# Eight token tiles of h = x2·w_in by Strassen products in pairs, wo2's blocks packed early and parked in DRAM, attention's steps reordered

## The chip, the cores and the metric

The kernel runs on one core of a Trainium2 chip. The metric is the device time of one launch in microseconds (us). An execution with a hardware profile gives the trace from which all durations below are read. The five engines run their own instruction streams in order and wait for each other by semaphores: PE (TensorE: matmuls and transposes), DVE (VectorE), ACT (ScalarE), POOL (GpSimd) and SP, which here only issues DMA transfers.

## What is computed

```python
x = attention(q, k, v)          # 2 batches, 8 heads, 576 tokens, 64 wide, with rotary angles
x = x.reshape(1152, 512)        # tokens x model width
a, b = x @ w_a, x @ w_b         # 1152 x 1536 each
x2 = (a * b) @ w_out            # 1152 x 512
h = x2 @ w_in                   # 1152 x 1024
solu = h * softmax(h)
ln = layernorm(solu) * g_ln
out = ln @ w_out2               # 1152 x 512
```

The matrices of weights come as 64-bit floats. For float32 accuracy a matmul operand is split in a high part (rounded to the matmul format fp32r) and a low part (the rest), and each product is three matmuls, high·high, high·low and low·high.

## The kernel before

**Order.** The whole program is one table of words, SCHEDULE (lines 36 to 140). A loop at the end of the function looks each word up in STEP or in a second table and calls the step, which emits instructions on its engines. An engine runs what was emitted for it in that order, so the table fixes each queue. A third number in a word (`gl.1.2.1`) puts a step's subtraction on POOL rather than DVE.

**Attention** (0 to 161 us) works on eight units u, each a batch and a pair of heads: loads of q, k and v by SP, rotary "ropes" on POOL and DVE (`rope`, L308, L313, L315; words rq and rk), transposes, scores (qk, L434), row maximum (mx, L443, DVE), exponentials (ex, L451, ACT), transposes of them (tp, L464), their high and low parts (ph on ACT, pl on DVE), and the product with v (pv, L513).

**Weights** come as 64-bit floats. `load_n` fetches one block of 128x1024, `Weights.pack` (L157) builds float32 from the two halves in three instructions of ACT (words pa, pb, pc) and three of DVE (the first, L170, is p2; then p3 and p4), `high` (hi, L181, ACT) writes the rounded part and `low` (lo, L184, DVE or POOL) the rest. Two raw buffers alternate, and `queue` sets the order of blocks: twelve pairs for w_a and w_b, six of w_out, four of w_in (h0 to h3), four of w_out2 (out0 to out3).

**FFN** (161 to 297 us): three of the twelve feature tiles are direct (L704), nine go by seven Strassen products each (`product`, L887).

**X stage** (297 to 378 us): x2 transposed, in three token groups t and twelve steps f. `g_hi` (gh, L936, ACT) and `g_lo` (gl, L734 through the helper tt_) split a·b, `x_mm` (X.t.f, L957) issues twelve matmuls, `x2_hi` (L965) and `x2_lo` (L969) write x2T's parts out of PSUM.

**h stage** (378 us to the end): for each of nine token tiles i of 128 tokens

```python
    def h_mm(i, kk):
        if kk == 0:
            ph[i] = ps_s.tile([P, 2, 512], F32, tag="s", name=f"h{i}")
        for xa, a in ((0, 0), (0, 1), (1, 0)):
            for c in range(2):
                nc.tensor.matmul(
                    ph[i][:, c], x2T[kk][:, xa, i * P:(i + 1) * P], W["h", kk].w[:, a, c * 512:(c + 1) * 512],
                    start=(kk == xa == a == 0), stop=(kk == 3 and xa == 1),
                )
```

that is 24 matmuls of 512 columns a tile (H.i.kk, L981), then the maximum (hx, L988, DVE), exponential (he, L993, ACT), multiplication (hm, L999, DVE), statistics (hs, DVE and one small POOL power, L1009), normalization (hn, L1014, DVE), transposes (L, L1022), their parts (lh on ACT, L1028; ll on DVE), the product with w_out2 (O, L1058) and the store. The four blocks of w_out2 are loaded and packed last, beside the end of the X stage and the start of the h stage.

Of the kernel before, what the change touches and what calls it, by code (L numbers as in the profile page):

```python
# [22 lines left out]
P = 128  # L23
NP = H // 2
# [10 lines left out]
NSTD = 3  # L35
SCHEDULE = """
cs.0 wm1.0 rka0.0 ll.0 rka1.0 rka2.0 kha.0 rqx0.0 rqx1.0 rqx2.0 rqa0.0 rqa1.0 kla.0 rqa2.0 qdx.0 qda.0 wm2.0
kA_0.0 rkb0.0 rkb1.0 kA_1.0 qAx0.0 qA_0.0 qAh0.0 rkb2.0 rqb0.0 lv.0 rqb1.0 khb.0 qAl0.0 R_0.0 qAh1.0 klb.0 R_1.0
R_2.0 wm3.0 qk.0 mx.0 rqb2.0 qdb.0 qAl1.0 wm4.0 qk.1 mx.1 kB_0.0 ex.0 qk.2 qB_0.0 mx.2 rq0.1.1 rk0.1.1 tp.0 ex.1
ex.2 rq1.1.1 kB_1.0 qB_1.0 rk1.1.1 qk.3 rq2.1.1 qk.4 mx.3 rk2.1.1 ex.3 ph.0 mx.4 pl.0 qB_2.0 tp.1 ph.1 t4A_0.0  # L40
t4A_1.0 qd.1 pl.1 qk.5 mx.5 vh.0 tp.2 qA_0.1 tp.3 ex.4 qk.6 kh.1 ph.2 ex.5 t4A_2.0 kl.1.1 t4R_0.0 pl.2 kB_0.1
vl.0.1 ph.3 ld.0 qA_1.1 mx.6 qk.7 qA_2.1 kB_1.1 tp.4 ex.6 pl.3 t4R_1.0 mx.7 lk.2 ph.4 tp.5 kA_0.1 t4R_2.0 R_0.1
rk0.2.1 pl.4 ph.5 pl.5 lq.2 rq0.2.1 qk.8 mx.8 pv00_0.0 rk1.2.1 kA_1.1 tp.6 ex.7 R_1.1 qk.9 R_2.1 rq1.2.1
pv01_0.0 lk.3 rk2.2.1 rq2.2.1 ex.8 qk.10 ph.6 mx.9 qB_0.1 pv00_1.0 pl.6 mx.10 sa.0 lv.1 ex.9 rs_0.0 qB_1.1 qk.11
lv.2 mx.11 pv01_1.0 ex.10 qk.12 lq.3 pv00_2.0 pv00_3.0 tp.7 pv01_2.0 kh.2 kl.2.1 pv01_3.0 qd.2 qB_2.1 mx.12
ex.11 ph.7 pl.7 rs_1.0 rs_2.0 t4B_0.0 qk.13 rk0.3.1 lk.4 tp.8 t4B_1.0 t4B_2.0 mx.13 ex.12 vh.1 ph.8 kA_0.2 tp.9
rk1.3.1 kA_1.2 pl.8 ph.9 pl.9 qk.14 qA_0.2 pv10_0.0 qA_1.2 qA_2.2 vl.1.1 mx.14 tp.10 tp.11 ex.13 pv10_1.0
rk2.3.1 ph.10 ph.11 pl.10 pv11_0.0 pv11_1.0 tp.12 pl.11 ex.14 pv10_2.0 t4R_0.1 pv10_3.0 qk.15 pv11_2.0 pv11_3.0
rq0.3.1 rq1.3.1 kB_0.2 t4R_1.1 ph.12 t4A_0.1 kh.3 kB_1.2 t4R_2.1 rq2.3.1 qd.3 t4A_1.1 qk.16 pl.12 tp.13 tp.14
mx.15 mx.16 pv00_0.1 kl.3.1 t4A_2.1 ex.15 qk.17 ph.13 pl.13 R_0.2 pv00_1.1 ph.14 pl.14 ex.16 tp.15 mx.17 R_1.2  # L50
# [1093 lines left out]
```

## Time and profile before

| | us |
|---|---|
| three runs | 485.25, 485.4, 486.24; median 485.4 |
| profiled execution | 484.92 |
| its span, first to last instruction | 483.1 |
| PE busy | 472.3 (98%) |
| DVE busy | 390.6 (81%) |
| ACT busy | 332.4 (69%) |
| POOL busy | 172.2 (36%) |

Busy times are sums over instructions; the granted TensorE clock was 0.99 to 1.00 of full speed throughout. The stretches in the rows further down are stages of the program, and a chain is followed back from the last instruction, each step to what released it.

### The profile page before, as it was taken

The numbers are of one execution on the slowest core, as the hardware profiler recorded it, in microseconds if no ns is written. First come the engines' busy times: TensorE is split into PE (matmuls) and PEld (weight loads), VectorE is DVE, ScalarE is ACT, GpSimd is POOL, SyncE is SP. The second block draws the span as 40 slices with busy tenths as digits, with TensorE's granted clock in tenths as the row PEclk, the third lists the DMA queues.
The fourth block names the chain that finished last, engine by engine and source line by source line (L and its number), as shares of the span: only waits on it lengthen the run. The fifth ranks groups of instructions, "written<-read, shape, count | busy, mean of one in ns | idle before, by whom it ended". The sixth has DMA issues, their size and how long they took to land.

```text
span 483.1 us, 8335 instructions
## 1 busy us (share of the span) xinstructions
PE 472.3 (98%) x3132; PEld 446.4 (92%) x3132; DVE 390.6 (81%) x582; ACT 332.4 (69%) x619; POOL 172.2 (36%) x138
## 2 busy tenths in 40 slices
PE   7899999999999999999999999999999999999997
PEld 7789999999989999999999999999999878888886
DVE  5789999999999898988886878786777888587441
ACT  4799999999998375777666668576767576133312
POOL 1999989969316002022221532020321202010000
PEclk9999999999999999999999999999999999999999
DMA  5642333421002523222422134423423200000012
GB/s 123 172 128 74 100 82 102 114 65 50 27 28 86 166 68 117 88 87 89 135 81 61 74 94 168 176 87 121 143 95 139 115 1 2 22 24 22 24 42 67
DMA packets 45779, 41.76 MB, mean 86 GB/s; under 512 B 23787, under 2 KB 40746, under 8 KB 45226
## 3 DMA queue, kind: packets, MB, share of 16 engines
q1 hardware_dynamic: 44794, 40.33, 27.0%
q10 hardware_dynamic: 944, 0.89, 0.6%
q8 instruction: 25, 0.41, 0.4%
q14 instruction: 16, 0.13, 0.1%
HBM read 36.92 MB, written 2.39 MB: 81 GB/s over the span
## 4 chain that ended last, share of the span: by engine, by line
PE 82%; DVE 10%; DMA 2%; issue 2%; POOL 2%; ACT 2%; SPq 1%; ACTq 0%; DVEq 0%; POOLq 0%
PE x L957 14%; PE out L1058 10%; PE pb L887 9%; PE ab L704 8%; PE h L981 7%; PE s L434 6%; PE pv L513 6%; PE pc L887 6%; PE pa L887 6%; PE t L464 5%; DVE nm L443 2%; PE lt L1022 2%; DMA kraw<-in_k_dram 1%; DVE pT L482 1%; DVE f L174 1%
## 5 line engine op out<-in xcount | busy, mean ns | idle before, releaser
L957 PE MATMUL x<-gs,wx 128*128 128x384 f32 x432 | 75.4, 334 | 0.0
L957 PEld LDWEIGHTS x<-gs,wx 128*128 128x128 f32 x432 | 74.9, 188 | 0.2
L434 PE MATMUL s<-kS,qS 128*128 128x288 f32 x320 | 59.6, 311 | 3.1 <-DVE qS L384 1.4
L443 DVE TENSOR_REDUCE nm<-s 128x1 f32<-128x576 f32 x72 | 54.0, 752 | 5.1 <-PE s L434 4.2
L451 ACT ACTIVATE e<-s,nm 128x576 f32<-128x576 f32 x72 | 53.7, 746 | 4.6 <-DVE nm L443 4.3
L164 ACT ACTIVATE f<-f 128x1024 f32<-128x1024 f32 x48 | 50.9, 1064 | 0.9
L981 PE MATMUL h<-wh,x2T 128*128 128x512 f32 x216 | 51.2, 392 | 0.2 <-DVE et L999 0.2
L434 PEld LDWEIGHTS s<-kS,qS 128*128 128x128 f32 x320 | 45.1, 188 | 6.1 <-ACT e L451 2.8
L482 DVE TENSOR_TENSOR pT<-t,pT 128x512 fp32r<-128x512 f32 x72 | 48.4, 684 | 0.8
L981 PEld LDWEIGHTS h<-wh,x2T 128*128 128x128 f32 x216 | 40.1, 188 | 8.6 <-PE h L981 0.6
L513 PE MATMUL pv<-pT,V 128*128 128x288 f32 x288 | 46.5, 301 | 0.0
L464 PE MATMUL t<-ident,e 128*128 128x128 f32 x288 | 42.6, 274 | 0.6 <-DVE pT L482 0.3
L478 ACT CAST pT<-t 128x512 fp32r<-128x512 f32 x72 | 41.2, 586 | 1.6 <-PE t L464 1.1
L513 PEld LDWEIGHTS pv<-pT,V 128*128 128x128 f32 x288 | 39.9, 188 | 0.5
L1058 PE MATMUL out<-wo,lnT 128*128 128x512 f32 (+1 forms) x180 | 39.8, 373 | 0.0
L1028 ACT CAST lnT<-lt 128x512 fp32r<-128x512 f32 x18 | 10.2, 589 | 40.6 <-PE lt L1022 40.6
L704 PE MATMUL ab<-xT,wab 128*128 128x384 f32 x216 | 38.1, 335 | 0.0
L734 POOL TENSOR_TENSOR gs<-g,gs 128x384 fp32r<-128x384 f32 x15 | 17.7, 1181 | 55.7 <-ACT gs L936 55.7
L704 PEld LDWEIGHTS ab<-xT,wab 128*128 128x128 f32 x216 | 37.4, 188 | 0.0
L464 PEld LDWEIGHTS t<-ident,e 128*128 128x128 f32 x288 | 33.9, 140 | 2.5 <-DVE pT L482 1.1
L1058 PEld LDWEIGHTS out<-wo,lnT 128*128 128x128 f32 x180 | 31.0, 189 | 5.3
L172 DVE SCALAR_TENSOR_TENSOR f<-raw,f 128x1024 int32<-128x1024 int32 x26 | 34.8, 1340 | 0.4
(181 smaller groups left out, 992.0 us busy)
## 6 DMA issues: line engine op xcount, KB each, us to landing
raw<-in_moe_w_out_dram SPq DMA_DIRECT2D x10, 1024.0 KB
raw<-in_moe_w_a_dram SPq DMA_DIRECT2D x12, 512.0 KB
raw<-in_moe_w_b_dram SPq DMA_DIRECT2D x24, 256.0 KB
raw<-in_moe_w_in_dram SPq DMA_DIRECT2D x4, 1024.0 KB
kraw<-in_k_dram SPq DMA_DIRECT2D x16, 128.0 KB
qd<-in_q_dram SPq DMA_DIRECT2D x16, 128.0 KB
vraw<-in_v_dram SPq DMA_DIRECT2D x8, 256.0 KB
qd<-qd SPq DMA_DIRECT2D x6, 288.0 KB
```

The lines of the kernel that those rows point to most:

```text
L164: act.activation(_raw(t), _raw(t), AF.Copy, scale=2.0 ** -SHIFT)
L434: nc.tensor.matmul(s[:, c, :KC], qS[u % 2][:, a, off:off + P], kS[u % 2][:, h, c * KC:(c + 1) * KC], start=(m == 0), stop=(m == last),)
L443: nc.vector.tensor_reduce(t, ps[n][:, :, :KC], axis=AX.XY, op=ALU.max, negate=True)
L451: nc.scalar.activation(t.rearrange("p (c n) -> p c n", c=2), ps.pop(n)[:, :, :KC], AF.Exp, bias=nm.pop(n), accum_out=sums[u][:, i:i + 1],)
L464: nc.tensor.transpose(t[:, j, :], e[n][:, j * P:(j + 1) * P], ident)
L482: nc.vector.tensor_tensor(lo, src, _raw(hi), op=ALU.subtract)
L513: nc.tensor.matmul(o[:, :KC], w[:, h, 4 if m == 8 else m % 4].rearrange("p a d -> p (a d)"), t[:, m, c * KC:(c + 1) * KC], start=(m == 0), ...
L704: nc.tensor.matmul(pab[f, t][:, m, :CW], wf[:, a, (kk, 4 + (kk + 2) % 4)[m], :], xT[kk][:, xa, t * CW:(t + 1) * CW], start=(kk == a == xa ...
L887: nc.tensor.matmul(dst[:, c, :KC], w[:, a, k * P:(k + 1) * P], x(k, xa)[:, c * KC:(c + 1) * KC], start=(fresh and k == a == xa == 0), stop ...
L957: nc.tensor.matmul(px[t, m][:, :CW], w[:, a], r[:, ga], start=(f == 0 and a == ga), stop=(f == NF - 1 and a == 1),)
L981: nc.tensor.matmul(ph[i][:, c], x2T[kk][:, xa, i * P:(i + 1) * P], W["h", kk].w[:, a, c * 512:(c + 1) * 512], start=(kk == xa == a == 0), ...
L1058: nc.tensor.matmul(po[i, part][:, cols], lnT[i][:, la, kk, :], w[:, a, cols], start=(kk == la == a == 0), stop=(kk == NK2 - 1 and la == 1),)
```

## The change

**h in pairs.** Tile 0 stays as it was (L1038). Tiles (1,2), (3,4), (5,6) and (7,8) go by Strassen: with the two tiles' rows, the two halves of the 512-wide sum and the two halves of h's 1024 columns as 2x2 blocks, seven products Q1 to Q7 (`h_product`, L1131) of 6 matmuls each give both tiles. The weight sums T are built once (`ht_sum`, words u1 to u4 on DVE, tile tfh; high parts `ht_hi`, L1060, ACT). Their low parts are made without a vector engine: ACT writes the negated high part (`ht_seed`, L1067), and a DMA issued by POOL adds the sum onto it (`ht_add`, L1070), four transfers of 512 KB from SBUF to SBUF. The sums S of x2's blocks are built for each pair (`hs_sum`, tile sf, DVE and POOL) and split (`sx_hi`, L1104, ACT; `sx_lo`). The first tile of a pair ends in PSUM (ph), the second in SBUF (hs), by two ACT copies and two DVE additions. One extra matmul (L1114) stands ahead of the first pair.

**w_out2 early.** out0 and out1 are loaded among the FFN's blocks, out2 and out3 ahead of w_in's. After packing and scaling, SP writes each as 512 KB to DRAM (`spill`, so, L784) and brings it back later (`bring`, ri, L789); `high_there` and `low_there` split it then.

**Buffers and order.** a·b's tile is six of two instead of two of six, x2T one tile, and all words of SCHEDULE stand in a new order, attention's too; four ropes move from POOL to DVE.

```diff
-rk0.2.1 pl.4 ph.5 pl.5 lq.2 rq0.2.1 qk.8 mx.8 pv00_0.0 rk1.2.1 kA_1.1 tp.6 ex.7 R_1.1 qk.9 R_2.1 rq1.2.1
+kA_0.1 kA_1.1 ex.7 qk.8 t4R_2.0 R_0.1 rq0.2.1 rk1.2 mx.8 pv00_0.0 R_1.1 qk.9 pv00_1.0 pl.4 ph.5 tp.6 rk2.2.1
...
-    queue = [("ab", f) for f in range(NF)]
-    queue += [("x", n) for n in range(6)] + [("h", n) for n in range(4)] + [("out", n) for n in range(4)]
+    queue = [("ab", f) for f in range(10)] + [("out", 0), ("ab", 10), ("out", 1), ("ab", 11)]
+    queue += [("x", n) for n in range(6)] + [("out", 2), ("out", 3)] + [("h", n) for n in (0, 2, 1, 3)]
...
+    def spill(n):
+        t = W[queue[n]].t
+        spilled[n] = dram.tile([P, 8 * P], F32, tag="wd", name=f"wd{n}", bufs=4)
+        nc.sync.dma_start(out=spilled[n], in_=_raw(t))
+
+    def bring(n):
+        w = W[queue[n]]
+        w.w = home(n)
+        nc.sync.dma_start(out=_raw(w.w[:, 1]), in_=spilled[n])
...
+            b11, b12, b21, b22 = (_raw(W["h", 2 * r + k].t)[:, c * 512:(c + 1) * 512] for r in range(2) for c in range(2))
+            dst, x, y = {1: (0, b12, b11), 3: (1, b22, b12), 2: (2, b22, t[:, 0]), 4: (3, b21, t[:, 2])}[j]
+            tt_(t[:, dst], x, y, sub, eng)
...
+    def ht_seed(k, j):
+        nc.scalar.activation(hT[k, j][:, 1], _raw(hT[k, j])[:, 0], AF.Copy, scale=-1.0)
+
+    def ht_add(k, j):
+        nc.gpsimd.dma_start(
+            out=_raw(hT[k, j])[:, 1].rearrange("p a n -> p (a n)"),
+            in_=tf2[k][:, 2 * j:2 * j + 2].rearrange("p a n -> p (a n)"), accum_op=ALU.add,
+        )
...
+            for k in range(2):
+                for xa, a in ((0, 0), (0, 1), (1, 0)):
...
+                    nc.tensor.matmul(
+                        dst, l, w, start=(fresh and k == xa == a == 0), stop=(k == 1 and xa == 1), skip_group_check=True
+                    )
...
+    def q_add(c):
+        def fn(i):
+            src = ph[i][:, 1] if c else pc2.pop(i)
+            nc.vector.tensor_tensor(hs[i][:, c], src, hs[i][:, c], op=plus)
+            if c:
+                ph[PAIRS[i]] = hs[i]
...
+        "Q1": h_product("a", (0, 0), (0, 0), True), "Q2": h_product("a", (1, 0), (1, 0)),
+        "Q3": h_product("b", 4, (1, 1)), "Q4": h_product("c", (1, 1), 4), "Q5": h_product("b", 1, 1),
+        "Q6": h_product("b", 2, 2), "Q7": h_product("c", 3, 3, True),
```

On PE, at the passage from the X stage to the h stage, the kernel before goes on with whole tiles (h_4709 is tile 1, h_4735 tile 2; gs is a·b's part, wh a block of w_in):

```order
L957 MATMUL x_3_4468<-gs_11_4617,wx_4269 128x384 x3
L981 MATMUL h_4709<-wh_4388,x2T_4414 128x512 x6
L981 MATMUL h_4709<-wh_4395,x2T_4416 128x512 x6
L981 MATMUL h_4709<-wh_4569,x2T_4411 128x512 x6
L981 MATMUL h_4709<-wh_4582,x2T_4422 128x512 x6
L981 MATMUL h_4735<-wh_4388,x2T_4414 128x512 x6
```

and the changed one runs tile 0 (h_4752), the extra matmul and the first products of the pair (h_4789 is tile 1, hc the third accumulator, hT the weight sums, sx the sums S):

```order
L1013 MATMUL x_3_4511<-gs_11_4670,wx_4231 128x384 x3
L1038 MATMUL h_4752<-wh_4493,x2T 128x512 x6
L1038 MATMUL h_4752<-wh_4655,x2T 128x512 x6
L1038 MATMUL h_4752<-wh_4519,x2T 128x512 x6
L1038 MATMUL h_4752<-wh_4672,x2T 128x512 x6
L1114 MATMUL h_4789<-wh_4493,x2T 128x512
L1131 MATMUL h_4789<-wh_4493,x2T 128x512 x3
L1131 MATMUL h_4789<-wh_4655,x2T 128x512 x3
L1131 MATMUL hc_4804<-hT_4523,sx_4740 128x512 x3
L1131 MATMUL hc_4804<-hT_4726,sx_4740 128x512 x3
L1131 MATMUL h_4789<-hT_4633,sx_4740 128x512 x3
L1131 MATMUL h_4789<-hT_4735,sx_4740 128x512 x3
```

Tile 0, which the kernel before has among the last steps of the X stage, comes behind it, and the weight sums hT_4726 and hT_4735 are wanted by the fourth and the sixth group behind tile 0.

On ACT the changed kernel makes those weight sums' parts at that passage (CAST on L1060 the high part, ACTIVATE on L1067 the negated copy, L1022 x2T's high parts, L992 a·b's, L192 w_in's):

```order
L1060 CAST hT_4633<-tfh_4490 128x1024
L1067 ACTIVATE hT_4633<-hT_4633 128x1024
L992 CAST gs_9_4638<-g_3725 128x384
L992 CAST gs_10_4652<-g_3921 128x384
L192 CAST wh_4655<-f 128x1024
L992 CAST gs_11_4670<-g_3921 128x384
L192 CAST wh_4672<-f 128x1024
L1022 ACTIVATE x2T<-x_0_4499 128x384
L1060 CAST hT_4726<-tfh_4721 128x1024
L1022 ACTIVATE x2T<-x_2_4507 128x384
L1067 ACTIVATE hT_4726<-hT_4726 128x1024
L1060 CAST hT_4735<-tfh_4721 128x1024
```

Behind it comes the negated copy for hT_4735; in the kernel before, ACT packs w_out2 at this place. POOL issues the adding DMA behind each negated copy.

On POOL, at the start of attention, the kernel before has these ropes (t2q and t2k the swapped products, qd and kraw the results, of units 0 and 1):

```order
L344 TENSOR_TENSOR kd_178<-kraw_104,kd_178 128x4x64
L315 TENSOR_TENSOR qd_105<-qd_105,t2q_0_215 128x4x64
L308 TENSOR_TENSOR t2q_1_285<-qd_168,s_sb 128x576
L308 TENSOR_TENSOR t2k_1_287<-kraw_172,s_sb 128x576
L313 TENSOR_TENSOR qd_168<-qd_168,c_sb 128x9x64
L313 TENSOR_TENSOR kraw_172<-kraw_172,c_sb 128x576
L315 TENSOR_TENSOR qd_168<-qd_168,t2q_1_285 128x9x64
L315 TENSOR_TENSOR kraw_172<-kraw_172,t2k_1_287 128x576
```

and the changed one these:

```order
L327 TENSOR_TENSOR qd_102<-qd_102,t2q_0_210 128x4x64
L356 TENSOR_TENSOR kd_169<-kraw_101,kd_169 128x4x64
L325 TENSOR_TENSOR qd_159<-qd_159,c_sb 128x9x64
L327 TENSOR_TENSOR kraw_163<-kraw_163,t2k_1_270 128x576
L327 TENSOR_TENSOR qd_159<-qd_159,t2q_1_258 128x9x64
```

Both swapped products and k's product with the cosines of unit 1 are DVE's now (of unit 2, one more).

## Rows read from the trace of the kernel before

**Rows 1.** Busy time of each engine by stage (length, PE PEld DVE ACT POOL, clock, DMA share, GB/s).

```profile
0.00:20.00 20.00, 16.09 (x116) 14.57 (x116) 11.87 (x29) 10.96 (x28) 10.20 (x14) 1.00 0.65 171
20.00:80.00 60.00, 58.26 (x466) 55.53 (x467) 56.67 (x97) 57.54 (x146) 56.70 (x45) 1.00 0.36 95
80.00:161.00 81.00, 79.62 (x630) 75.65 (x630) 78.79 (x134) 73.80 (x184) 48.71 (x39) 1.00 0.22 59
161.00:297.50 136.50, 136.50 (x965) 136.35 (x965) 116.66 (x147) 93.69 (x121) 30.12 (x17) 1.00 0.33 109
297.50:366.00 68.50, 68.50 (x397) 68.50 (x396) 50.45 (x59) 49.21 (x70) 14.66 (x13) 1.00 0.35 124
...
378.00:440.00 62.00, 61.78 (x293) 51.12 (x292) 48.96 (x77) 29.46 (x45) 9.18 (x8) 1.00 0.04 15
440.00:483.10 43.10, 39.52 (x213) 33.69 (x211) 18.07 (x32) 9.99 (x19) 1.65 (x3) 0.99 0.14 39
```

**Rows 2.** Chain that ended last, from the X stage on (start, length, what).

```profile
297.54 68.66 PE x L957 x396
...
402.04 5.46 PE h L981 x24
...
471.03 8.50 PE out L1058 x60
```

**Rows 3.** Groups by line and shape: busy us, mean ns, idle before.

```profile
L172 DVE SCALAR_TENSOR_TENSOR f<-raw,f 128x1024 int32<-128x1024 int32 x26 | 34.8, 1340 | 0.4
...
L174 DVE SCALAR_TENSOR_TENSOR f<-raw,f 128x1024 int32<-128x1024 int32 x26 | 33.3, 1281 | 0.5
...
L170 DVE TENSOR_SCALAR f<-f 128x1024 int32<-128x1024 int32 x26 | 20.6, 795 | 7.5 <-ACT f L164 7.5
...
L734 DVE TENSOR_TENSOR gs<-g,gs 128x384 fp32r<-128x384 f32 x21 | 12.5, 600 | 7.6 <-ACT gs L936 7.6
...
L1014 DVE TENSOR_SCALAR et<-et,mv,rs 128x1024 f32<-128x1024 f32 x9 | 9.4, 1039 | 2.9 <-POOL rs L1009 2.9
...
L965 ACT ACTIVATE x2T<-x 128x384 fp32r<-128x384 f32 x12 | 5.5, 488 | 0.9 <-PE x L957 0.9
L734 DVE TENSOR_TENSOR tf<-f 128x512 f32<-128x512 f32 x8 | 5.5, 690 | 0.3
...
L734 DVE TENSOR_TENSOR tf<-f,tf 128x256 f32<-128x256 f32 x13 | 5.5, 420 | 0.2
...
L184 DVE TENSOR_TENSOR wh<-f,wh 128x1024 fp32r<-128x1024 f32 x4 | 4.9, 1218 | 0.2 <-ACT wh L181 0.2
...
L181 ACT CAST wh<-f 128x1024 fp32r<-128x1024 f32 x4 | 4.2, 1052 | 0.0
```

**Rows 4.** POOL's timeline early in attention (start, length, engine, instruction).

```profile
12.13 1.41 POOL L308 TENSOR_TENSOR t2q<-qd,s_sb 128x576 f32<-128x576 f32 x1
...
18.99 1.42 POOL L315 TENSOR_TENSOR kraw<-kraw,t2k 128x576 f32<-128x576 f32 x1
```

**Rows 5.** SP's timeline: one block of w_out, 1 MB, is issued.

```profile
353.70 0.38 SPq L229 DMA_DIRECT2D raw<-in_moe_w_out_dram  x1
```

**Rows 6.** Busy time by microsecond behind that issue, columns as in rows 1.

```profile
354.00:355.00 1.00, 1.00 (x8) 1.00 (x7) 0.56 (x1) 0.58 (x2) 0.35 (x1) 1.00 0.09 33
...
356.00:357.00 1.00, 1.00 (x7) 1.00 (x6) 0.58 (x2) 1.00 (x3) 0.00 (x0) 1.00 1.02 422
...
358.00:359.00 1.00, 1.00 (x8) 1.00 (x7) 0.96 (x2) 0.81 (x2) 0.51 (x1) 1.00 0.01 4
```

**Rows 7.** Chain that ended last, in attention: a small transfer.

```profile
69.17 2.50 DMA rd<-rr
```

**Rows 8.** DVE's timeline at one place of the h stage.

```profile
381.29 2.89 DVE L1014 TENSOR_SCALAR et<-et,mv,rs 128x1024 f32<-128x1024 f32 x1 [0.67 <-POOL rs L1009]
```

**Rows 9.** POOL's timeline at the same place.

```profile
381.23 2.41 POOL L184 TENSOR_TENSOR wo<-f,wo 128x1024 fp32r<-128x1024 f32 x1
```

**Rows 10.** Waits of 0 to 161 us (total, times, longest).

```profile
DVE nm L443 <- PE s L434: 4.2, 8, 0.8
```

More of the change, by code (lines that the diff above doesn't have):

```diff
@@ L46 @@
[L46 to L50, printed above, removed]
@@ L199, in attention_gated_ffn_solu_ffn @@
     xp = ctx.enter_context(tc.tile_pool(name="xp", bufs=1))
-    xT = [xp.tile([P, 2, NT], F32R, tag=f"x{m}", name=f"xT{m}") for m in range(NP)]
+    x_all = xp.tile([P, NP, 2, NT], F32R, tag="x", name="xT")
+    xT = [x_all[:, m] for m in range(NP)]
     NF = DF1 // P
@@ L726, in to_ffn @@
         pools["a"] = sctx.enter_context(tc.tile_pool(name="ps_a", bufs=1, space=PSUM))
[L727 to L728 removed]
+        for f in range(0, 6, 2):
+            g_tile(f)
+        sums_f = [gpool.tile([P, 2, 2, S], F32, tag=f"g{3 + j}", name=f"sums_f{j}") for j in range(3)]
         sums_x = sp.tile([P, 3, 2, 2, S], F32R, tag="s", name="sums_x")
@@ L962, in x2_hi @@
     def x2_hi(t, m):
-        if x2T[m] is None:
-            x2T[m] = xp.tile([P, 2, NT], F32R, tag=f"x{m}", name=f"x2T{m}")
+        if not x2T:
+            pools["x2"] = x2 = xp.tile([P, 4, 2, NT], F32R, tag="x", name="x2T")
+            x2T.extend(x2[:, k] for k in range(4))
         nc.scalar.activation(x2T[m][:, 0, t * CW:(t + 1) * CW], px[t, m][:, :CW], AF.Copy, scale=UP ** -2)
@@ new lines, in attention_gated_ffn_solu_ffn, with sx_src, sx_dst, sx_hi @@
+    SX = {3: 2, 2: 0, 1: 1, 4: 3}
+    def sx_src(i, q):
+        return sf[i][:, q in (1, 4), :, q != 4]
+    def sx_dst(i, q, a):
+        return sx[i][:, SX[q], a].rearrange("p (k n) -> p k n", k=2)
+    def sx_hi(i, q):
+        if i not in sx:
+            sx[i] = pools["l"].tile([P, 4, 2, 2 * P], F32R, tag="S", name=f"sx{i}", bufs=1)
+        nc.scalar.copy(sx_dst(i, q, 0), sx_src(i, q))
+    def sx_lo(i, q, eng=0):
+        tt_(sx_dst(i, q, 1), sx_src(i, q), _raw(sx_dst(i, q, 0)), sub, eng)
@@ new lines, in h_product @@
+    def h_product(name, left, right, fresh=False):
+        def fn(i):
+            if name == "a" and fresh:
+                ph[i] = ps_s.tile([P, 2, 512], F32, tag="s", name=f"h{i}")
+                if i == min(PAIRS):
+                    nc.tensor.matmul(ph[i][:, 1], x2T[0][:, 0, 0:P], W["h", 0].w[:, 0, 0:512], start=True, stop=True)
+            if name == "c" and fresh:
+                pc2[i] = ps_o.tile([P, 512], F32, tag="o", name=f"hc{i}")
+            dst = pc2[i] if name == "c" else ph[i][:, "ab".index(name)]
+            for k in range(2):
+                for xa, a in ((0, 0), (0, 1), (1, 0)):
+                    if isinstance(left, int):
+                        l = sx[i][:, SX[left], xa, k * P:(k + 1) * P]
+                    else:
+                        h, second = left
+                        r = (PAIRS[i] if second else i) * P
+                        l = x2T[2 * h + k][:, xa, r:r + P]
+                    if isinstance(right, int):
+                        w = hT[k, right in (2, 4)][:, a, right in (3, 4)]
+                    else:
+                        h, c = right
+                        w = W["h", 2 * h + k].w[:, a, c * 512:(c + 1) * 512]
+                    nc.tensor.matmul(
+                        dst, l, w, start=(fresh and k == xa == a == 0), stop=(k == 1 and xa == 1), skip_group_check=True
+                    )
+        return fn
@@ new lines, in q_seed, with q_copy, fn @@
+    def q_seed(i):
+        nc.scalar.copy(ph[i][:, 1], ph[i][:, 0])
+    def q_copy(c):
+        def fn(i):
+            if i not in hs:
+                hs[i] = pools["h"].tile([P, 2, 512], F32, tag="hs", name=f"hs{i}")
+            nc.scalar.copy(hs[i][:, c], pc2[i] if c else ph[i][:, 1])
+        return fn
+    def q_add(c):
+        def fn(i):
+            src = ph[i][:, 1] if c else pc2.pop(i)
+            nc.vector.tensor_tensor(hs[i][:, c], src, hs[i][:, c], op=plus)
+            if c:
+                ph[PAIRS[i]] = hs[i]
+        return fn
```

305 lines of the change are left out of this document (187 added, 118 removed).

## The prediction, made before the run

> **What bounds the kernel now.** I read the busy times by stage first, then the chain, then the durations by shape, then single places of the timelines.
>
> By stage [rows 1], PE is busy for 136.50 of 136.50 us in the FFN, 68.50 of 68.50 in the X stage and 61.78 of 62.00 in the h stage up to 440 us. The last window has 39.52 us of matmuls, and the chain's last piece of PE, 8.50 us from 471.03 [rows 2], ends at 479.53: that window too is full until PE has nothing left. From 161 us to the end PE's own work is the bound, and what leaves PE there leaves the time, as long as nothing makes it wait. In attention PE is busy for 153.97 of 161 us, DVE for 147.33 [rows 1]; from 20 us on DVE idles only 3.33 + 2.21 = 5.5 us, of which 4.2 behind scores [rows 10]. There DVE and PE bound together, and POOL is full until 80 us (56.70 of 60).
>
> The time is the profiled execution's: 484.92, span 483.1. The median of the three runs, 485.4, stands 0.48 above it; I add that at the end. About 0.2% (1.0 us) is what a measurement of this kernel can tell from no change.
>
> **Part 1: fewer matmuls in h.** Before, nine tiles of 24 make 216. After, tile 0 has 24, four pairs have 7 products of 6, that is 168, and one extra stands ahead: 193, so 23 less. They have the same 512 columns. In the chain 24 of them take 5.46 us [rows 2], 0.2275 each: 23 x 0.2275 = **5.2 us** off PE, all of it in the part that PE bounds.
>
> **Part 2: the sums that pay for it.** Per pair, DVE and POOL build 8 sums S and 4 low parts, ACT 4 high parts and three copies, DVE two additions of 128x512 (0.69 [rows 3]). All four blocks of w_out2 are packed earlier; a block costs DVE 0.80 + 1.34 + 1.28 = 3.42 us [rows 3]. DVE by stage: the FFN takes in two blocks (6.8) and some four low parts and products that POOL had, about 1 us each: from 116.7 [rows 1] to about 127.6, of 136.5 of PE. The X stage takes in the weight sums, 8 x 0.69 = 5.5, and a few more low parts (0.60, 1.22 [rows 3]): from about 56 to 64, of 75 up to tile 0's maximum. The h stage loses two packings (6.8) and gains 8 additions (5.5) and some 5 us of sums: from about 71 to 74, of 98. ACT grows by 14 and 11 us in the first two stages and stays at least 20 under PE in the FFN; in X it comes to 74 with 75 there, where not all of it is due at X's end. POOL goes from about 11 us in the last two windows [rows 1] to 27.5. Every engine stays under PE in each stage, so I price these sums at nothing; the cover is 9 us of DVE in the FFN, which would be gone if DVE ran 7% slower there.
>
> **Part 3: the passage from X to h.** Before, tile 0's matmuls lay among X's last ones. Now they come behind them, and the second half of the weight sums is made just there. Count from the end of X's last matmul. X's matmuls take 68.66/396 = 0.173 us each [rows 2]. PE then has four groups of 6 for tile 0 (5.45 us), the extra one and Q1 (1.6), one group on hT_4523 (0.7): **hT_4726 is wanted at 7.7 us, hT_4735 at 9.1.** On ACT, the first high part of x2T waits for nine matmuls before the end (-1.56) and takes 0.49 [rows 3]; then high part 1.05, x2T 0.49, negated copy 1.05, high part 1.05, copy 1.05 [rows 3]: the two adding DMAs can be issued at about 1.5 and 3.6. DVE has the sums ready in time: it starts 24 matmuls before the end (-4.2), where a ring buffer comes free, and needs 0.69, 0.42 and four times 0.69, so it ends near -0.3. From issue to landing, then, **6.2 and 5.5 us are covered by PE's own work.**
>
> What such a DMA takes no row shows: POOL issues none in this trace. Bounds: a small transfer took 2.50 us [rows 7]; 1 MB issued at 353.70 [rows 5] had its last byte by about 358.0 [rows 6], 4.4 us, of which 1.2 us was before the first byte and the rest at up to 422 GB/s. An adding transfer of 512 KB moves its bytes three times (two reads, one write): 1.5 MB at that rate is 3.7, and with 1.2 ahead about 5. So 2.5 to 5; I take 4.4, the nearest row by bytes, which is under the cover: **no stall.** The Trainium skill ("DMA: Bandwidth & Descriptors", section on the anatomy of a DMA of the software path) puts such a transfer at about 2.0 us + bytes/436 GB/s; by that it would be an estimated 3.2 us, and the sum the same.
>
> Smaller waits are there by the order: the copy of Q1's result for a seed stands behind the exponential of tile 0 on ACT (about 0.3 of wait on PE), tile 3's first product waits until tile 0's multiplication frees PSUM (about 0.2), and some 0.3 for the other pairs. These are guesses from 0 to 2; I take **+0.8.** At the end, tile 8's normalization is ready some 14 us after the last product (two tiles' maximum to normalization in series on DVE, the last of PE's sums in SBUF) and its transposes come at 15.4 in PE's order, 1.4 us later: nothing.
>
> **Part 4: w_out2 through DRAM.** Four writes and four reads of 512 KB, beside a DMA share of 0.33 to 0.35 [rows 1]. The first block is wanted by a matmul more than 15 us after its read is issued, against 4.4 for a transfer of 1 MB: nothing. SP has little behind these issues but stores.
>
> **Part 5: attention's order.** Four ropes leave POOL (4 x 1.42 = 5.7 us), which has them without a gap from 12.13 to 20.4 us [rows 4]. On DVE they cost about 0.75 each (a sum of 512 columns takes 0.69 [rows 3], a rope has 576), 3.0 in all; three of the four fall between 12 and 20 us, where DVE idles (11.87 of 20 busy [rows 1]), one where it doesn't. The matmuls, maxima and exponentials are the same, only interleaved otherwise. Against: at most the 3.0. For: at most what waits for POOL until 80 us, some 3 to 4 of PE's 3.91 + 1.74 = 5.7 idle us there [rows 1]. I take **0**, and keep -3 to +3.
>
> Sum: 484.92 - 5.2 + 0.8 + 0 = 480.5; with the 0.48 above, **481.0 us.**
>
> **Rivals.**
>
> (a) *The adding DMAs land late, and the change is slower.* The two tiles that they read from share one buffer: the second half's sums on DVE wait until the first half's DMAs have landed, and the second half's DMAs follow. The first pair is issued between 9 and 7.4 us before the end of X. A landing time L within 5 us costs nothing; beyond, both delays add, and PE stalls about 2L - 11. The gain of 4.4 is gone, and this decides, from L = 8 us on; with L = 10 it is +9, **490.** For it: no row has such a transfer, DVE and POOL work without a pause there. Against: 1 MB took 4.4.
>
> (b) *Attention's order costs more than 3 us.* DVE idles only 5.5 us from 20 us on; an order in which maxima come later behind scores doubles the 4.2 us of that wait [rows 10], and with the rope about +5: **486.** Against it, PE's and DVE's streams are otherwise the same.
>
> (c) *Attention gains more than 3 us.* POOL, full until 80 us, was what loads and keys waited for; with 5.7 us less there PE's idle time shrinks: -4, **477.**
>
> (d) *DVE and POOL disturb each other.* Where both ran, DVE's normalization took 2.89 us [rows 8] beside a subtraction of POOL of 2.41 [rows 9]; the other eight average (9.4 - 2.89)/8 = 0.81 [rows 3]. POOL's work in the h stage grows two and a half times. Eight such meetings are up to 17 us on DVE, which idles 13 us until 440 [rows 1] and 25 behind; so most is covered, and 1 to 3 us show at the passage or at the end: **483.** The Trainium skill ("SBUF — State Buffer", section "Who interferes with whom") says that a DVE instruction in its two-port mode and GpSimd block each other fully, and that one with two SBUF inputs contends with GpSimd's reads; the pair of rows agrees with the first, and by the second the new sums S, all from SBUF, would meet too.
>
> (e) *It doesn't save what it counts*: PE idles for the seeds and additions of each pair, four times 1.5 us: **486.**
>
> **How the numbers follow.** Forecast (478 to 484): 0.63, nearly all faster by over 0.2% (0.62, and 0.01 same). (a) 0.11: 0.03 faster, 0.02 same, 0.06 slower. (b) 0.08: 0.02 same, 0.06 slower. (c) 0.07, faster. (d) 0.06: 0.04 faster, 0.01 each of the others. (e) 0.05: 0.01 same, 0.04 slower. Sum: faster 0.76, same 0.07, slower 0.17. The range leaves out about half of (a) and little of the rest above, and the far end of (c) below: **476.5 to 487.0.**
>
> **What would show it.** The first matmul of X at the same time as before within 3 us (part 5). h's matmuls at 193 and PE some 5 us shorter. Behind X's last matmul, PE without a pause over 0.5 us up to the first product on hT_4735, and the second half's adding DMAs landing within 5.5 us of their issue (part 3). DVE under PE in the FFN, with X's start as far from the end of attention as before, 136.4 us (part 2). The prediction is wrong if the FFN and X stages get longer by over 2 us, if PE has stalls of over 2 us before the pairs' products, or if attention moves by over 3.

## The result and the profile after

The change made the kernel slower: 488.48 us (median of six runs, 488.14 to 490.23) against 485.48 (six runs, 485.05 to 486.24), a ratio of 1.0061 with a 95% interval of 1.0043 to 1.0079. The forecast was 481.0, with a range of 476.5 to 487.0. The profiled execution took 488.67, its span is 486.6, against 484.92 and 483.1 before.

By stage the changed kernel reads as follows (busy time of each engine; columns as in [rows 1], the last four windows cut where its stages lie):

```profile
0.00:20.00 20.00, 17.17 (x122) 15.81 (x122) 14.81 (x34) 11.79 (x30) 6.89 (x12) 1.00 0.54 124
20.00:80.00 60.00, 58.12 (x464) 55.28 (x465) 57.91 (x97) 57.26 (x145) 53.73 (x42) 1.00 0.40 105
80.00:161.00 81.00, 79.01 (x624) 74.70 (x623) 78.28 (x134) 72.74 (x183) 50.27 (x40) 1.00 0.23 63
161.00:297.50 136.50, 135.15 (x951) 134.23 (x950) 122.93 (x152) 100.73 (x130) 26.45 (x18) 1.00 0.39 129
297.50:371.00 73.50, 73.50 (x428) 73.36 (x428) 56.66 (x73) 60.25 (x84) 16.66 (x13) 1.00 0.49 155
371.00:396.00 25.00, 21.18 (x94) 17.66 (x93) 22.80 (x29) 12.10 (x20) 14.55 (x14) 0.93 0.41 106
396.00:440.00 44.00, 43.43 (x210) 35.86 (x209) 38.92 (x65) 20.09 (x39) 19.52 (x19) 1.00 0.05 19
440.00:486.60 46.60, 42.65 (x227) 36.38 (x225) 27.22 (x47) 14.66 (x29) 7.38 (x10) 1.00 0.13 34
```

Attention takes as long as before. Two stages that were full on PE no longer are: the FFN, 135.15 of 136.50 us, and the passage to the h stage, 21.18 of 25.00 and the only stretch with a granted clock under full speed (0.93). Before, the stretch of the passage was:

```profile
371.00:396.00 25.00, 24.78 (x119) 20.96 (x118) 21.80 (x33) 16.84 (x24) 3.49 (x3) 1.00 0.23 85
```

PE's timeline of the changed kernel shows where (start, length, matmuls; in brackets what the group waited for):

```profile
239.03 1.85 PE L943 MATMUL pc<-xT,wT 128*128 128x288 f32 x12 [0.63 <-ACT p L956]
...
287.87 1.85 PE L943 MATMUL pb<-xT,wB 128*128 128x288 f32 x12 [0.52 <-DVE p L972]
289.93 1.86 PE L943 MATMUL pa<-xT,wB 128*128 128x288 f32 x12 [0.20 <-ACT pb L952]
...
299.76 0.51 PE L1013 MATMUL x<-gs,wx 128*128 128x384 f32 x2
...
374.64 5.64 PE L1038 MATMUL h<-wh,x2T 128*128 128x512 f32 x24
380.12 0.39 PE L1114 MATMUL h<-wh,x2T 128*128 128x512 f32 x1
...
381.71 1.52 PE L1131 MATMUL hc<-hT,sx 128*128 128x512 f32 x6
387.05 2.31 PE L1131 MATMUL h<-hT,sx 128*128 128x512 f32 x6 [3.82 <-ACT h L1138]
389.16 3.87 PE L1131 MATMUL h<-wh,x2T 128*128 128x512 f32 x12
392.87 1.52 PE L1131 MATMUL h<-hT,sx 128*128 128x512 f32 x6
...
409.50 0.66 PE L1193 MATMUL lt<-ident,et 128*128 128x128 f32 x4 [0.57 <-DVE et L1185]
```

With the same marks in the trace of before, the difference of the spans, 3.5 us, is accounted for:

| from, to (on PE) | before | after | difference |
|---|---|---|---|
| start to the first Strassen product of the FFN | 192.67 | 192.67 | 0 |
| to the first matmul of X | 104.71 | 107.09 | +2.4 |
| to the end of X and tile 0's h | 80.42 | 80.36 | -0.1 |
| to the last matmul | 101.73 | 102.55 | +0.8 |
| to the end | 3.57 | 3.90 | +0.3 |

What stands behind the second line shows at the first of the three waits in the FFN. On ACT the read-out that PE waits for (L956, word o7.6, 0.64 us) stands behind the high part of a weight sum (L890, word th.7):

```profile
237.40 1.05 ACT L890 CAST wT<-tf 128x1024 fp32r<-128x1024 f32 x1
238.34 0.64 ACT L956 COPY p<-pc 128x576 f32<-128x576 f32 x1
```

The fourth line of the table hides two large terms. The 23 matmuls that are gone are 5.2 us; against them stand the wait of 3.82, a clock that fell behind it (the 18 matmuls from 387.05 to 392.87 took 5.82 us, where 18 x 0.2275 would be 4.1: 1.7 more), and the wait of 0.57: 6.1 together.

**What PE waited for at 387.05.** The product Q6 of the first pair adds onto a copy that ACT makes (L1138). On ACT the copy stands behind the exponential of tile 0, that one waits for tile 0's maximum on DVE, and on DVE the maximum stands behind a sum of x2's blocks, S2b (L747, sf). DVE's timeline there:

```profile
378.67 0.42 DVE L747 TENSOR_TENSOR sx<-sf,sx 128x256 fp32r<-128x256 f32 x1
379.19 4.95 DVE L747 TENSOR_TENSOR sf<-sf,x2T 128x256 f32<-128x256 f32 x1
384.06 1.21 DVE L1159 TENSOR_REDUCE mx<-h 128x1 f32<-128x1024 f32 x1
```

and POOL's:

```profile
378.62 0.88 POOL L1070 DMA_DIRECT2D hT<-tfh  x1 [0.20 <-POOL sf L747]
379.23 1.59 POOL L747 TENSOR_TENSOR sf<-x2T 128x512 f32<-128x512 f32 x1
380.49 1.03 POOL L747 TENSOR_TENSOR sx<-sf,sx 128x256 fp32r<-128x256 f32 x1
381.18 2.67 POOL L747 TENSOR_TENSOR wout<-wout 128x1024 fp32r<-128x1024 f32 x1
384.22 0.72 POOL L747 TENSOR_TENSOR sf<-x2T,sf 128x256 f32<-128x256 f32 x1 [0.37 <-DVE sf L747]
```

A DVE sum of 256 columns, 0.43 us for the same step of the second pair, lasted 4.95: it began 40 ns ahead of three POOL instructions without a gap and ended 0.3 us after the last of them. The instructions of both engines read two operands from SBUF each. And just ahead of that run POOL had issued the last adding DMA, which was then in flight. So there are two suspects: POOL's run and the DMA.

The adding DMAs themselves landed in time. In the page's list of DMA issues the last column is the median from issue to landing:

```profile
hT<-tfh POOLq DMA_DIRECT2D x4, 512.0 KB, 5.0
```

The four took 4.6 to 5.4 us. The last one, issued at 378.62, landed at 383.76, 5.1 us later, under the 5.5 that PE's work was to cover.

### The profile page after: what moved, and what is told of

It reads as the page before. It is cut to its first block, busy times and chain, and to the rows that moved or that the text cites. A ratio compares the mean times of both kernels' runs of the same rounds, so it can differ in the third digit from the quotient of the medians.

```text
span 486.6 us, 8468 instructions
## 1 busy us (share of the span) xinstructions
PE 470.2 (97%) x3109; PEld 443.3 (91%) x3109; DVE 419.5 (86%) x624; ACT 349.6 (72%) x655; POOL 195.5 (40%) x164
## 4 chain that ended last, share of the span: by engine, by line
PE 69%; DVE 14%; ACT 5%; POOL 3%; DMA 3%; issue 3%; SPq 0%; ACTq 0%; POOLq 0%; DVEq 0%
PE x L1013 15%; PE out L1229 10%; PE ab L716 8%; PE pb L943 7%; PE pc L943 5%; PE pa L943 5%; PE h L1131 5%; PE pv L525 5%; PE s L446 4%; PE t L476 3%; DVE nm L455 2%; DVE sf L747 2%; DVE pT L494 2%; PE lt L1193 2%; PE hc L1131 1%
## 5 line engine op out<-in xcount | busy, mean ns | idle before, releaser
L446 PE MATMUL s<-kS,qS 128*128 128x288 f32 x320 | 58.6, 309 | 1.6 <-ACT e L463 1.6
L1229 PE MATMUL out<-wout,lnT 128*128 128x512 f32 (+1 forms) x240 | 51.8, 372 | 0.0
L1229 PEld LDWEIGHTS out<-wout,lnT 128*128 128x128 f32 x240 | 41.3, 189 | 7.2
L179 DVE SCALAR_TENSOR_TENSOR f<-raw,f 128x1024 int32<-128x1024 int32 x26 | 32.3, 1244 | 0.5
L747 POOL TENSOR_TENSOR gs<-g,gs 128x384 fp32r<-128x384 f32 x10 | 10.9, 1090 | 53.2 <-ACT gs L992 34.3
L177 DVE SCALAR_TENSOR_TENSOR f<-raw,f 128x1024 int32<-128x1024 int32 x26 | 31.8, 1221 | 0.4
L943 PE MATMUL pa<-xT,wB 128*128 128x288 f32 x216 | 31.7, 295 | 0.2 <-ACT pb L952 0.2
L943 PE MATMUL pb<-sums_x,wT 128*128 128x288 f32 x216 | 31.6, 295 | 0.0
```

The costliest lines, as they stand in the source:

```text
L446: nc.tensor.matmul(s[:, c, :KC], qS[u % 2][:, a, off:off + P], kS[u % 2][:, h, c * KC:(c + 1) * KC], start=(m == 0), stop=(m == last),)
L943: nc.tensor.matmul(dst[:, c, :KC], w[:, a, k * P:(k + 1) * P], x(k, xa)[:, c * KC:(c + 1) * KC], start=(fresh and k == a == xa == 0), stop ...
L1229: nc.tensor.matmul(po[i, part][:, cols], lnT[i][:, la, kk, :], w[:, a, cols], start=(kk == la == a == 0), stop=(kk == NK2 - 1 and la == 1),)
```

## Experiments at the passage: POOL's run or the DMA

Theory A: POOL's back-to-back sums hold DVE up. Rival B: the adding DMAs do.

**POOL emptied (a_pool_empty).** In SCHEDULE, three POOL steps go behind S4a and S4b, which wait for S2b:

```diff
-hx.0 Sh.1.2 S1a.3.1 Sl.1.1.1 he.0 Sl.1.2 xl.2.1 Q1.1 ri.10 lj.12.1 q1.1 S4a.1.1 hj.10 S4b.1.1 Q7.1
+hx.0 Sh.1.2 he.0 Sl.1.2 xl.2.1 Q1.1 ri.10 q1.1 S4a.1.1 hj.10 S4b.1.1 Sl.1.1.1 S1a.3.1 lj.12.1 Q7.1
```

> Three POOL steps (S1a.3, Sl.1.1 and the low part of w_out2's block, lj.12) stand behind S4b.1 instead of ahead of it, so that POOL has nothing to run while DVE makes S2b of the first pair. Theory A (DVE's sum of two SBUF tiles is held up by POOL's back-to-back sums): that sum takes 0.4 to 0.6 us instead of 4.95, PE's wait ahead of Q6 of the first pair falls from 3.8 to under 0.5 us, the clock stays up, the time falls by about 5 us, to 483 to 484. Rival B (the adding DMAs, landing at that time, hold DVE up): the sum still takes 3 to 5 us and the time stays within 1.5 us of 488.5.

Measured: 484.06 us (10 runs) against 485.47 for the kernel before in the same series, ratio 0.9968 (0.9953 to 0.9983). DVE's sum, with the DMAs as they were:

```profile
378.94 0.43 DVE L741 TENSOR_TENSOR sf<-sf,x2T 128x256 f32<-128x256 f32 x1
```

PE has no wait at all ahead of Q6 and the clock of 371 to 396 us is 1.00. One move of three words gives 4.4 us back by the medians; from X's first matmul to the last matmul the two traces have 177.9 us against 182.9, 5.0 less. POOL's run is necessary for the hold-up.

**The longest of the three moved (b_lj_late).** Only `lj.12.1` goes behind `S4b.1.1`.

> Only the longest of the three POOL steps, lj.12 (2.67 us), is moved behind S4b.1. Theory A: DVE's sum ends when POOL's Sl.1.1 does, so it takes about 2.3 us instead of 4.95, PE's wait falls by about 2.7 us to some 1.2, the time to 484 to 486. Rival B: the sum stays at 3 to 5 us and the time within 1.5 us of 488.5.

Measured: 485.6 us, ratio 1.0001 (0.9986 to 1.0016). DVE's sum and POOL's two instructions:

```profile
379.33 2.62 DVE L741 TENSOR_TENSOR sf<-sf,x2T 128x256 f32<-128x256 f32 x1
```
```profile
379.37 1.60 POOL L741 TENSOR_TENSOR sf<-x2T 128x512 f32<-128x512 f32 x1
380.63 1.02 POOL L741 TENSOR_TENSOR sx<-sf,sx 128x256 fp32r<-128x256 f32 x1
```

Here too the sum ends 0.3 us behind POOL's run, of two instructions now, and not with the last adding DMA, which landed at 383.92. PE's wait is 1.49 us and the clock doesn't fall.

**Without the DMAs (c_no_dma).** The negated copies go and two subtractions on DVE take the DMAs' place:

```diff
-un.1.0 S1a.1 ua.1.0 S1b.1 uh.1.1 un.1.1 S2a.1.1 lo.25 Sh.1.3 Sh.1.1 ua.1.1
+S1a.1 ul.1.0 S1b.1 uh.1.1 S2a.1.1 lo.25 Sh.1.3 Sh.1.1 ul.1.1
```

> The second half's two adding DMAs and negated copies are replaced by two subtractions on DVE (1.2 us each); POOL's other steps stay. Theory A: DVE's S2b of the first pair still ends only when POOL's run of sums ends, so it takes over 1.5 us wherever the two overlap, and PE's wait stays at 3 us or more. Rival B: with no DMA in flight the sum takes 0.4 to 0.6 us.

Measured: 488.88 us in one run. The sum took 0.78 us, though POOL ran one instruction beside it and the next behind; but DVE's own 2.4 us of subtractions came later instead, PE waited 0.95 and 2.23, and nothing was gained. It moved both engines' times and did not settle the question.

**The DMAs left out, all else in place (e_no_add).** The words `ua.1.0` and `ua.1.1` are deleted; the pairs of h then lack the weight sums' low parts.

> The second half's two adding DMAs are left out (the negated high parts stay where the low parts should be, so h's pairs lose that correction); POOL's run of sums and DVE's order stay. Theory A in its plain form (POOL's back-to-back sums alone hold DVE up): DVE's S2b of the first pair takes over 3 us as before, PE waits over 2.5 us ahead of Q6, the time is 487 to 489. Rival B' (POOL's run holds DVE up only while an adding DMA is in flight or being issued): the sum ends at the first boundary between POOL's instructions, under 2 us, and the time falls to 484 to 486.

Measured: 485.81 us in one run. DVE's sum and POOL's same three instructions:

```profile
381.26 0.78 DVE L741 TENSOR_TENSOR sf<-sf,x2T 128x256 f32<-128x256 f32 x1
```
```profile
379.57 1.30 POOL L741 TENSOR_TENSOR sf<-x2T 128x512 f32<-128x512 f32 x1
380.82 0.93 POOL L741 TENSOR_TENSOR sx<-sf,sx 128x256 fp32r<-128x256 f32 x1
381.71 2.58 POOL L741 TENSOR_TENSOR wout<-wout 128x1024 fp32r<-128x1024 f32 x1
```

It began inside POOL's second instruction and got in at that one's end, although the third followed at once. DVE's step just ahead of it, a low part of the same size (0.42 in the changed kernel), began inside POOL's first instruction and got in at that one's end:

```profile
379.79 1.37 DVE L741 TENSOR_TENSOR sx<-sf,sx 128x256 fp32r<-128x256 f32 x1
```

So theory A in its plain form fell: the run alone costs DVE one instruction of POOL, not three. But without the DMAs the run also began earlier, so DVE's sum started inside it rather than just ahead of it.

**The start moved (h_phase).** One word, `xl.2.1`, goes ahead of `S2b.1`, so that DVE's sum starts inside POOL's first instruction, with the DMAs in place.

> One word is moved: DVE writes a low part of x2T (xl.2.1, 0.5 us) ahead of the first pair's S2b instead of behind it, so that S2b begins inside POOL's first sum instead of 40 ns ahead of it; the adding DMAs and POOL's run stay. Theory A' (a DVE sum that begins inside a POOL instruction gets in at that one's end, one that begins just ahead of POOL's run waits for all of it): S2b takes 0.9 to 1.7 us, PE's wait ahead of Q6 falls from 3.8 to 0.5 to 1.5 us, the time to 484 to 485.5. Theory B' (an adding DMA in flight is what keeps DVE out between POOL's instructions): S2b still ends with POOL's run, 4 to 4.6 us, time 488 to 489.

Measured: 489.68 us (4 runs), ratio 1.0080 (1.0063 to 1.0097). DVE's sum, and POOL's run, inside whose first instruction it began:

```profile
381.02 4.57 DVE L741 TENSOR_TENSOR sf<-sf,x2T 128x256 f32<-128x256 f32 x1
```
```profile
380.68 1.60 POOL L741 TENSOR_TENSOR sf<-x2T 128x512 f32<-128x512 f32 x1
381.94 1.03 POOL L741 TENSOR_TENSOR sx<-sf,sx 128x256 fp32r<-128x256 f32 x1
382.64 2.66 POOL L741 TENSOR_TENSOR wout<-wout 128x1024 fp32r<-128x1024 f32 x1
```

Theory A' fell: a sum that starts inside the first instruction was held to the run's end too, where without the DMAs a step that started there got in at its end (1.37 above). PE waited 3.82.

**Only the last DMA left out (n_one_add).** `ua.1.1` is deleted, so hT_4735 lacks its low part.

> Of the changed kernel's second half, the last adding DMA alone is left out (hT_4735's low part stays a negated copy); the one before it, issued 2.9 us ahead of DVE's S2b, and POOL's run of sums stay. If the adding DMA issued directly ahead of the run is what keeps DVE out between POOL's instructions: S2b takes under 1.7 us, the time 484 to 486. If any adding DMA in flight does: S2b ends with POOL's run or with that DMA's landing, 2 to 4.5 us, the time 486.5 or more.

Measured, one run: DVE's sum took 0.78 us, PE's wait ahead of Q6 was 0.60. The time, 489.17, missed the forecast: this execution had reached the first product of the FFN at 195.88 rather than 192.67, 3.2 us later, and took 1.05 more for X. Together: **POOL's run and an adding DMA issued directly ahead of it are both needed.** With either gone the sum takes 0.43 or 0.78; with both it waits for the whole run. The adding DMA that was left, issued 3.8 us ahead of the sum with another POOL sum between it and the run, was still in flight (380.57 to 385.31) and doesn't do it. Whether the nearness of the DMA in time or in POOL's queue is what counts was not tried. One more sign is open: in the runs that held DVE up, the records of POOL's successive instructions overlap by 0.3 us, in those that let it in by 0.05; no run tells whether that is a cause or goes along with it.

## Experiments in the FFN: too full, or in the wrong order

Theory F: DVE and ACT are too full with w_out2's two blocks. Theory G: the steps' new order brings a product close behind the read-out that it waits for.

**Two blocks not packed (d_no_pack).** All words pa to p4 and sc of blocks 10 and 12 are deleted, so w_out2's first two blocks are not converted.

> The packing and scaling of w_out2's first two blocks is left out (they are loaded, written to DRAM and brought back unpacked). Theory F (the FFN's stalls come from these two packings on ACT and DVE): X's first matmul starts at 297.4 to 298 us instead of 299.8, the time falls by about 2.4, to 486. Rival G (the new order of the FFN's other steps, or a cover that was already gone): X's first matmul stays behind 299 us and the time above 487.5.

Measured: DVE is busy 115.47 us and ACT 90.72 of the 136.50, both less than before the change [rows 1], and yet PE waits in the FFN: 0.63 and 0.55 at the first two of the three places as before, none at the third, and 0.64 at a new one (280.33). First product to first X took 107.7. Theory F fell in its simple form. (492.0 in one run; 2 us of it before the first product.)

**Three steps moved (f_ffn).** `o7.6` goes ahead of `th.7`, `o5.10` ahead of `tl.11`, `o1.11` ahead of `pa.15`.

> In the FFN alone, three steps move ahead of longer ones on their engine: o7 of tile 6 ahead of th of tile 7 on ACT, o5 of tile 10 ahead of tl of tile 11 on DVE, o1 of tile 11 ahead of a packing on ACT. Theory G (the FFN's stalls come from the new order, where a product's accumulator is wanted soon after it was filled and its copy stands behind other work): the three waits (0.63, 0.52, 0.20) go, first product to first X falls from 107.1 to 105.0 to 105.8 us, the time to 486.5 to 487.5. Theory F (the vector engines are simply too full there): waits of the same sum come up elsewhere in the FFN, 107.1 stays within 0.4 us and the time within 0.8 us of 488.5.

Measured: 491.06 us (4 runs), ratio 1.0113 (1.0100 to 1.0127). The three waits are gone and two new ones of 1.37 us each are there, at 244.75 (for o5 of tile 6, on DVE) and at 295.84 (for o6 of tile 11, on ACT behind packings). First product to first X: 108.05, worse by 1.0; the passage was as in the changed kernel (a wait of 3.82), with a granted clock of 0.86 from 371 to 396 us instead of 0.93. With POOL emptied as well (**g_both**):

> POOL emptied while DVE makes the first pair's S2b, and the three FFN moves, together. If both causes are right they add: 484.06 less 1 to 2 us, so 482.0 to 483.2, faster than the kernel before by 2 to 3.5 us. If the FFN's stalls only move elsewhere, 483.7 to 484.5.

484.87 us (12 runs), ratio 0.9996 (0.9975 to 1.0016): the passage's gain stands, the FFN's loss too.

**A second try (i_ffn2),** with POOL emptied and seven words put behind the read-outs that f_ffn had run into (`p4.8`, `gl.0.1` behind `o5.6`; `pb.16`, `pc.16`, `p2.16`, `p3.16`, `ld.17` behind `o6.11`):

> POOL emptied while DVE makes the first pair's S2b, the three FFN moves, and with them the work that the moves ran into put behind: a packing step, a low part of a*b and two packings of a w_out block stand behind o5 of tile 6 and o6 of tile 11. Theory G': first product to first X is 105.0 to 106.0 us (107.1 in the changed kernel, 108.05 with the three moves alone, 104.7 before), the time 482.3 to 483.6, faster than the kernel before by 1.8 to 3 us. Theory F (too full): new waits take the place of these, 106.8 or more, 483.8 to 485.

490.01 us, ratio 1.0094 (1.0079 to 1.0110): the packing on ACT put behind o6 came later, and with it DVE's steps of the same packing, which stand ahead of o5 of tile 11 in its queue; PE waited 3.57 for that, and 0.27 and 0.95 at tile 7. One of these DVE steps took 3.26 us instead of 1.22, beside a subtraction of POOL.

**Products swapped at one place (j_first).** On top of POOL emptied, P5 of tile 6 stands ahead of P4, so that P4 wants its accumulator 1.6 us later:

```diff
-th.7 tl.7 o7.6 p4.8 t1.8.1 P4.6 o4.6 ld.10 gl.0.1 gs P5.6 o1.7 pa.9 pb.9 P2.7 pc.9 o5.6 P3.6
+th.7 tl.7 o7.6 p4.8 t1.8.1 P5.6 o5.6 P4.6 o4.6 ld.10 gl.0.1 gs o1.7 pa.9 pb.9 P2.7 pc.9 P3.6
```

> On top of the kernel with POOL emptied (484.06): in the FFN product P5 of tile 6 and its read-out o5 stand ahead of P4, so that P4 follows P7 two products later and its wait for o7 (0.63) has 1.6 us more. Theory G (order, not fullness): first product to first X falls from 107.05 to 106.0 to 106.4 us and the time by 0.7 to 1.0, to 483.1 to 483.4. Theory F (the vector engines are too full, a wait that goes comes back): 106.8 or more, time unchanged or longer.

Measured: **483.2 us** (8 runs) against 485.98 in the same series, ratio 0.9952 (0.9934 to 0.9971). First product to first X: 105.99 against 107.05 with POOL emptied alone, as theory G had it: a wait of 0.63 less gave 1.06 back. This is the fastest kernel of the study and beats both. Against POOL emptied alone (0.9968, 0.9953 to 0.9983) the intervals overlap; that this edit gains rests on the traces, and l_two below, which has it and k_end has not, is again 1.08 shorter there (108.43 against 109.51).

**The FFN's end mended (k_end, l_two, m_three).** k_end moves o5 and o1 ahead and puts block 16's packing behind tile 11's read-outs; l_two adds j_first's edit; m_three puts the three DVE steps of that packing behind o4 and g0 as well.

> On top of the kernel with POOL emptied (484.06): at the FFN's end o5 of tile 10 stands ahead of tl of tile 11, o1 of tile 11 ahead of a packing, and the packing of one w_out block (pb, pc, p2, p3, p4 of block 16) behind o6, o7 and o5 of tile 11. Theory G: the two waits there (0.52 and 0.20, 1.2 us with the restarts) go, first product to first X is 105.8 to 106.2 us, the time 482.8 to 483.3. Theory F: the packings that were put behind delay X's own steps or the waits come back, 106.8 or more, time 484 or more.

> Both of these FFN edits with POOL emptied. Theory G: first product to first X 104.9 to 105.4 us, the time 481.9 to 482.5, some 3 us faster than the kernel before. Theory F: 106.5 or more, time 484 or more.

> As the kernel with both FFN edits (487.25), but the three DVE packing steps of block 16 stand behind o4 of tile 11 and the product behind it (g0), so that X's first matmul no longer waits for o4 behind them. Theory G (order): first product to first X 104.8 to 105.4 us, no wait of PE over 0.3 us from the FFN to X's first steps, time 481.6 to 482.6. Theory F (too full): a wait of 1 us or more comes back, at X's fifth step (which needs block 16) or at X's start, and the time is 483 or more.

Measured: 489.22 (ratio 1.0061, 1.0040 to 1.0082), 487.25 (1.0028, 1.0013 to 1.0044) and 486.7 (1.0021, 1.0010 to 1.0033). In k_end and l_two the two waits at the end are gone and one comes in their place, at X's first matmul, for o4 of tile 11 behind the packing; in k_end:

```profile
302.96 37.22 PE L1007 MATMUL x<-gs,wx 128*128 128x384 f32 x204 [3.68 <-DVE u L961]
```

More than half of this wait is another meeting of DVE and POOL. A DVE step of the packing, 1.22 us elsewhere, took 3.29 beside POOL's subtraction for w_out's block before it, and o4 stands behind it:

```profile
297.60 3.29 DVE L171 SCALAR_TENSOR_TENSOR f<-raw,f 128x1024 int32<-128x1024 int32 x1
```
```profile
297.16 2.65 POOL L189 TENSOR_TENSOR wx<-f,wx 128x1024 fp32r<-128x1024 f32 x1 [6.29 <-ACT wx L186]
```

The same stands in l_two (3.29), and in i_ffn2 it is the step of 3.26.

In m_three first product to first X is 104.57 us, without any wait (before: 104.71); but now X's own first steps are late, and X takes 80.14 us to its last matmul instead of 75.05:

```profile
306.58 0.44 PE L1007 MATMUL x<-gs,wx 128*128 128x384 f32 x1 [2.56 <-ACT gs L986]
307.38 70.37 PE L1007 MATMUL x<-gs,wx 128*128 128x384 f32 x395 [0.35 <-DVE gs L741]
```

What follows: at tile 6 the order was the cause, and an edit of the order removes the wait. At the FFN's end each of four edits removed the wait and got a larger one back within 20 us; there the packings, tile 11's read-outs and X's first splits want the same stretch of ACT and DVE, and POOL's subtraction held a DVE step up by 2 us in three of the kernels, by 0.9 in m_three. No edit tried kept a gain there, and whether one exists is open.

## Why the prediction was wrong

The measured time lies 7.5 us above the forecast. Two steps failed: the path from DVE to PE at the passage, which was taken to cost 0.3 us and cost 5.0 to 5.5, and the FFN's added work, which was priced at nothing and cost 2.4. Two of the prediction's own signs of being wrong came: the FFN and X stages longer by over 2 us, and a stall of over 2 us before a pair's product.

**Part 1 (23 matmuls, 5.2 us): right.** From the end of tile 0's h to the last matmul the changed kernel needs 0.8 us more with 6.1 us of waits and slow clock in it, so 5.3 less of work. In a_pool_empty, without that wait, the stretch takes 97.5 us against 101.7 before.

**Part 2 (sums and packings at nothing): wrong, by 2.4 us.** The step that failed is "every engine stays under PE in each stage, so I price these sums at nothing". The sums themselves were near: DVE 122.93 us in the FFN's window, ACT 100.73, both below the forecast. But a busy share says nothing of where in a queue a short read-out stands that PE waits for. The forecast had looked through the order at the passage and not in the FFN; the waits there, 0.63, 0.52 and 0.20, come to 1.35 and cost 2.4 with what PE loses around each; m_three, without them, needs 104.57 for that stretch, as the kernel before.

**Part 3 (passage): the DMA's price near, the wait missed.** The adding DMAs were put at 4.4 us, within 2.5 to 5; they took 4.6 to 5.4 and cost PE nothing. In a_pool_empty the last one landed at 383.51, some 0.2 us ahead of the matmuls on its tile, so rival (a) stayed away by little. The 3.2 us that the prediction estimates from the Trainium skill were too low. Of the smaller waits, put at 0.8 together, the term of 0.3 for Q1's copy behind tile 0's exponential is the one that failed: at this very copy PE waited 3.82, because tile 0's maximum, and with it the exponential, stood behind S2b on DVE, which part 3 does not have. The others came as 0.57. The mechanism is that of rival (d), at a price of "1 to 3 us" too small. It took one meeting of the old trace, 2.89 against 0.81 [rows 8, 9], about one POOL instruction, as the size of each. Here the meeting lasted three POOL instructions, 4.5 us, and stood on a chain of DVE, ACT and PE that let 3.8 of it through, and the clock fell behind PE's pause: 5.5 us by these terms, 5.0 by a_pool_empty. The Trainium skill ("SBUF — State Buffer", section "Who interferes with whom") says that a DVE instruction with two SBUF inputs contends with GpSimd's reads; the trace agrees, 4.95 against 0.42. It also says, of DVE's two-port mode, that whoever issues first gets the shared pair for the whole instruction. Here DVE's sum, not of that mode, had started 40 ns first by the trace and waited; at 376.60 a DVE subtraction with two SBUF operands had started 0.35 us first, took its usual 1.22, and POOL's sum beside it took 1.47 instead of 0.72.

**Part 4 (DRAM): right.** No wait for a block that was brought back shows.

**Part 5 (attention at 0): right for the two profiles compared,** 192.67 us to the first product in both. That they agree so closely is chance. The other profiles with this attention had the mark between 192.45 and 195.88; whether the new order is somewhat slower on average than the old, of which there is one profile, is open.

Rivals (b), (c) and (e) did not come. By the sum: 480.5 forecast for the profiled execution, plus 2.4 in the FFN and 5.0 to 5.5 at the passage, is 487.9 to 488.4; it was 488.67.

## What to carry to other kernels

A stage in which PE is busy all the time hides work by its place in the queue, not by its sum: before pricing added work at nothing, list for each short read-out that PE waits for what now stands ahead of it, and what that waits for. When sums go to POOL, look at which DVE instructions with two SBUF operands fall beside a run of POOL without gaps, above all behind a DMA that POOL itself has issued, and keep that run off the chain that feeds PE. A move that removes a wait is worth only what is left after the next late step: in the FFN one such edit, at tile 6, kept its gain and the others paid it back.

## What the runs showed of the hardware that was not expected

- With an adding DMA issued by POOL directly ahead, DVE's addition from two SBUF tiles waited through two or three POOL instructions, 2.62 and 4.95 us; without that DMA it got in at the end of the one in which it began, 0.78; without POOL's run it took 0.43 with the same DMAs.
- A DVE packing step that began 0.4 us inside a single POOL subtraction took 3.29 us instead of 1.22 (k_end), and got in at that one's end.
- The record of issuing one adding DMA of 512 KB on POOL lasts 0.87 to 1.02 us; at the passage POOL's next instruction began 0.6 us behind its start. From issue to landing it took 4.6 to 5.4.
- With PE's pause of 3.82 us the granted clock of 371 to 396 us was 0.93 in the changed kernel and in h_phase, 0.86 in f_ffn and d_no_pack; with pauses of 0.95 and 2.23 in c_no_dma it was 0.93, with one of 1.49 in b_lj_late 1.00.
